# V, U and S matmuls on 16-bit operands: x, w_in, v and w_spatial as float16 hi and lo behind scales worked out on the chip

## The chip, the core and the metric

The kernel runs on one core of a Trainium2 chip. A core has a matrix engine (TensorE, in the profile PE for matmuls and PEld for weight loads), a vector engine (VectorE, DVE), a scalar engine (ScalarE, ACT), a general engine (GpSimd, POOL) and a queue engine (SyncE, SP) that issues loads and stores. Each engine works through its own instructions in order, and waits on semaphores for the others. The metric is the device time of one execution in microseconds, as the median of several.

## The reference, cut to what matters

For eight batches, eight heads, 576 positions and a head width of 64, an attention with two parts is computed, and its result goes through a gated block:

```python
q_d, k_d, v_d = means of q, k, v over groups of 4 positions      # 144 positions
out_up    = repeat(softmax(q_d k_d^T / 8) v_d, 4)                # per head
out_local = softmax(where(|i-j| < 4, q k^T / 8, -1e9)) v         # a narrow band
x = (out_up + out_local) as (576, 512) per batch

h = relu(x @ w_in)                       # w_in 512 x 1024
u, v = h[:, :512], h[:, 512:]
v_n = (v - mean(v)) / sqrt(var(v) + 1e-6)           # per position
v_s = w_spatial @ v_n + b_spatial[:, None]          # w_spatial 576 x 576
out = (u * v_s) @ w_out                             # w_out 512 x 512
```

Inputs and output are float32; w_in and w_out come as float64 and are rebuilt on the chip from their integer words.

## The kernel before

**Attention.** One unit of work is a pair of heads; each of the eight batches has four pairs (`attention(n)`, n from 0 to 31). A pair loads q and k (L515) and v in overlapping windows (L521, L523), sums q and k over four positions (sum, L531 and L534), computes banded scores (S, L563, with the mask added as a bfloat16 matmul, L556), maximum, difference, exponential (L604), sum, reciprocal and norm (L608), transposes (L616) and values (AV, L696). Beside it runs the part on means: scores (L628), exponential (L637), norm (normd, L649 on ScalarE or L651 elsewhere), transposes (L664), values (L682). The mean of v is added up by DMAs that accumulate, issued by POOL (L504). Both parts meet in xf (L706, L708), which is split into x: hi = xf rounded (xhi, L713), lo = xf - hi (xlo, L715).

**Gated block.** `gated(b)` works on the x of a batch's four pairs. All its operands are held as two float32r tiles, hi and lo, and every product is three matmuls (hi hi, hi lo, lo hi). V (L742, and L747 for the last 64 positions): 128 positions by 512 columns, 12 matmuls a piece; then relu (L759), mean and variance (L751 to L753), the reciprocal root as a power on POOL (rstd, L769), apply (L756), vhi (L773) and vlo (L775, L781). U (L796): 128 features by 256 or 320 positions, 12 matmuls, relu into u (L799). S (L814, L816, L817): w_spatial times normalised v, 14 matmuls of 256 or 320 columns with the bias in the last, then gate (L825: u times S), ghi and glo (L827, L821). O (L844, L849): the gated values times w_out, 512 columns, copied out (L854) and stored.

**Weights.** 17 pieces are loaded at the start through two staging places `stg` (L391), which are handed out in the order V half of w_in (4), U half (4), w_spatial (5 and the bias), w_out (4). A float64 piece is rebuilt in six steps on VectorE, ScalarE and, for some, POOL (L406 to L431; the last is m3); hi and lo are then made at once (L379, L382).

**Order.** `Plan.run` writes out one order for each engine ahead of time: it lists the operations with planned durations, and always takes, of those that can start soonest (within NEAR ns), the one of lowest rank. Ranks are pair numbers plus constants per kind, three each (batch 0, batch 1, later): RANK, MRANK, WRANK. ON holds, by pair or piece, which engine does a movable operation (D VectorE, P POOL, A ScalarE; beyond its end the last letter holds). Places (`places`) are buffers; an operation that needs one waits until an earlier user is done. Where the plan leaves TensorE idle in the first 110 us it puts in bfloat16 matmuls without use (warm, L882). Nothing is reordered while the kernel runs.

Of the kernel before, what the change touches and what calls it, by code (L numbers as in the profile page):

```python
# [76 lines left out]
class Plan:  # L77
# [54 lines left out]
    def run(self, near=150.0, stay=0.0, dma=(1500.0, 4.2, 500.0), emit=True):  # L132
# [16 lines left out]
        while left:  # L149
# [89 lines left out]
RANK = {"load": [-6.425, 5.791, -0.091],  # L239
        "tv": [-13.62, 1.562, -8.346],  # L240
        "sum": [7.232, 2.664, -2.313],
        "S": [-5.456, -8.108, -3.65],
        "E": [-2.935, 8.439, 4.083],
        "N": [-20.365, 3.051, 3.136],
        "T": [3.06, 5.617, -6.295],
        "Sd": [-18.648, -4.028, 1.939],
        "Nd": [-2.732, 2.402, -1.457],
        "Td": [7.722, -5.93, 1.317],
        "AVd": [-13.128, 1.0, 1.083],
        "AV": [-1.585, -10.971, -1.682],  # L250
        "X": [-1.109, -4.0, 4.59]}
# [12 lines left out]
NEAR = 120.124  # L264
STAY = 7.582
# [14 lines left out]
def tile_kernel(ctx, tc, qk, vw, v4, w_in, wT, bsp, w_out, out, emit=True):  # L280
# [51 lines left out]
    win = const.tile([P, NC, 2, 2 * FF], F32R, name="win")  # L332
    wsp = const.tile([P, NT, 2, S], F32R, name="wsp")
    wsp_hh = const.tile([P, S], F32R, name="wsp_hh")
    wsp_lb = const.tile([P, S], F32R, name="wsp_lb")
    wo = const.tile([P, NF, 2, E], F32R, name="wo")
    sel = const.tile([P, 1], F32, name="sel")
    vt2 = const.tile([P, FF], F32R, name="vt2")
# [4 lines left out]
    plan.tag("stg", [stg[:, 0], stg[:, 1]])  # L343
# [5 lines left out]
    places("v", 3, [P, NW, D], F32)  # L349
# [27 lines left out]

    def split(dst_hi, dst_lo, src, scale, toks, rank, n, key):
        plan.op("ACT", 25 + act(n), lambda: nc.scalar.activation(dst_hi, src(), AF.Copy, scale=scale),  # L379
                r=toks, w=[("whi", key)], rank=rank, name="whi")  # L380
        plan.op("DVE", dve(n),
                lambda: nc.vector.scalar_tensor_tensor(dst_lo, src(), scale, f(dst_hi), op0=ALU.mult, op1=ALU.subtract),  # L382
# [3 lines left out]
    def fetch(parts, rank, kb):  # L386
        t = plan.buf("stg")
# [7 lines left out]
    def piece64(src, dst_hi, dst_lo, rank, key):  # L395

        t = fetch([(src, 0)], rank, 512)
        eb, mb = plan.buf("row"), plan.buf("row")
# [28 lines left out]
        def m3():  # L427
            if pr.eng == "POOL":
                nc.gpsimd.tensor_tensor(mb.ap, mb.ap, eb.ap, op=ALU.mult)
            else:  # L430
                nc.vector.scalar_tensor_tensor(mb.ap, mb.ap, 2.0**-20, eb.ap, op0=ALU.mult, op1=ALU.mult)  # L431
# [15 lines left out]
    def piece_tail(rank):  # L447
# [4 lines left out]
        def go():  # L452
            nc.scalar.copy(wsp_hh, t.ap[:, :S])
# [474 lines left out]
```

## Time and profile before

| | us |
|---|---|
| median of 3 runs | 614.08 |
| lowest and highest | 610.75 and 616.07 |
| the profiled execution | 617.94 |
| its span, first to last instruction | 616.0 |

The profile is of one execution. Its page gives busy time by engine, slices over the span, the chain of work that ended last, and groups of instructions named by line, engine and tile. A line such as `282.73 2.80 PE pmc L742 x12` of the chain says: from 282.73 us on, for 2.80 us, twelve matmuls of line 742 into tile pmc. In brackets behind an instruction stands how long its engine was idle before it, and who ended the wait. The mean granted TensorE clock of the execution was 0.983 of full speed.

### The profile page before, as it was taken

What the parts mean: (1) busy time and instruction counts of PE and PEld (TensorE: products, weight loads), DVE (VectorE), ACT (ScalarE), POOL (GpSimd) and SP (SyncE); (2) the same over time, 40 slices, a digit from 0 to 9 for tenths busy, and PEclk for the clock granted to TensorE, in tenths of its full rate; (3) what the DMA queues carried; (4) which work ended last, traced back from release to release, by engine and by line L of the source; (5) the groups of instructions that cost most, each with busy time, mean ns of one, the idle gap of its engine ahead of it and who ended that gap; (6) DMA issues with size and microseconds to landing.
All of it is one profiled execution on the core that took longest, in us unless ns stands there. A gap on an engine that the chain in (4) does not pass through costs nothing.

```text
span 616.0 us, 14561 instructions
## 1 busy us (share of the span) xinstructions
PE 590.8 (96%) x5987; PEld 518.0 (84%) x5987; DVE 400.7 (65%) x915; ACT 309.5 (50%) x793; POOL 183.0 (30%) x185
## 2 busy tenths in 40 slices
PE   6688888999999999999999999999999999999997
PEld 2556777898999889898999889898899889898895
DVE  5899779894696477478547857478557857135230
ACT  2666566764564446445635646444545545324221
POOL 2552441035322243114512343113522233114100
PEclk9889979999999999999999999999999999999999
DMA  9886652253234502336022622226112300000102
GB/s 261 248 209 147 156 168 92 82 151 58 78 101 88 173 14 62 95 98 144 14 65 78 194 49 61 79 87 156 20 58 95 117 9 24 18 18 2 52 1 77
DMA packets 37382, 56.95 MB, mean 92 GB/s; under 512 B 3650, under 2 KB 24130, under 8 KB 37316
## 3 DMA queue, kind: packets, MB, share of 16 engines
q1 hardware_dynamic: 35012, 48.94, 25.3%
q0 software_dynamic: 2304, 7.08, 7.4%
q8 instruction: 47, 0.77, 0.5%
q14 instruction: 19, 0.16, 0.1%
HBM read 46.57 MB, written 9.44 MB: 91 GB/s over the span
## 4 chain that ended last, share of the span: by engine, by line
PE 85%; DVE 7%; ACT 3%; DMA 2%; issue 1%; POOL 1%; SPq 0%; ACTq 0%; POOLq 0%
PE pmc L844 6%; PE pmb L814 5%; PE pmb L796 4%; PE pmd L796 4%; PE pmd L814 4%; PE pma L814 4%; PE pma L844 4%; PE pmd L742 4%; PE pma L742 4%; PE pmc L814 3%; PE pmc L796 3%; PE pma L796 3%; PE pmb L844 3%; PE pmb L742 3%; PE pmc L742 3%; PE pmd L844 2%
## 5 line engine op out<-in xcount | busy, mean ns | idle before, releaser
L844 PE MATMUL pmc<-wo,ga 128*128 128x512 f32 x132 | 33.0, 399 | 0.0
L814 PE MATMUL pmb<-wsp,vha 128*128 128x320 f32 (+1 forms) x204 | 30.8, 299 | 0.0
L814 PE MATMUL pma<-wsp,vha 128*128 128x256 f32 (+1 forms) x204 | 30.4, 297 | 0.0
L814 PE MATMUL pmd<-wsp,vha 128*128 128x256 f32 (+1 forms) x192 | 29.4, 304 | 0.0
L844 PEld LDWEIGHTS pmc<-wo,ga 128*128 128x128 f32 x132 | 24.3, 188 | 5.9 <-issue 0.6
L814 PEld LDWEIGHTS pmb<-wsp,vha 128*128 128x128 f32 x204 | 28.5, 188 | 0.1
L814 PEld LDWEIGHTS pma<-wsp,vha 128*128 128x128 f32 x204 | 28.0, 188 | 0.2 <-issue 0.2
L814 PEld LDWEIGHTS pmd<-wsp,vha 128*128 128x128 f32 x192 | 27.4, 196 | 0.5 <-issue 0.4
L651 POOL TENSOR_TENSOR edb<-edb,smdb 96x432 f32<-96x432 f32 x13 | 16.9, 1298 | 28.7 <-DVE smdb L642 23.6
L814 PE MATMUL pmc<-wsp,vha 128*128 128x256 f32 (+1 forms) x168 | 25.2, 299 | 0.0
L651 POOL TENSOR_TENSOR eda<-eda,smda 96x432 f32<-96x432 f32 x12 | 13.9, 1158 | 31.5 <-DVE smda L642 16.7
L814 PEld LDWEIGHTS pmc<-wsp,vha 128*128 128x128 f32 x168 | 23.1, 189 | 0.1
L844 PE MATMUL pma<-wo,ga 128*128 128x512 f32 x84 | 21.1, 400 | 0.0
L504 POOL DMA_DIRECT2D tvb<-v_dram x12 | 10.8, 903 | 33.7 <-DMA tvb<-v_dram 28.7
L504 POOL DMA_DIRECT2D tva<-v_dram x12 | 10.6, 884 | 33.0 <-DMA tva<-v_dram 23.1
L715 POOL TENSOR_TENSOR xa<-xfa,xa 128x576 fp32r<-128x576 f32 x7 | 10.2, 1460 | 33.4 <-ACT xa L713 33.4
L882 PE MATMUL pma<-mask_b,mask_a 128*128 128x512 bf16 x51 | 16.5, 457 | 3.2 <-DVE mask_a L329 3.2
L844 PEld LDWEIGHTS pma<-wo,ga 128*128 128x128 f32 x84 | 15.3, 188 | 3.5 <-issue 0.4
L582 DVE TENSOR_TENSOR sa<-sa,mxa 128x640 f32<-128x640 f32 x12 | 17.4, 1452 | 0.3
L715 POOL TENSOR_TENSOR xf<-xfa,xf 128x576 fp32r<-128x576 f32 x3 | 4.3, 1427 | 43.8 <-ACT xf L713 43.8
L594 DVE TENSOR_REDUCE smb<-sb 128x10 f32<-128x640 f32 x16 | 13.0, 814 | 4.5 <-ACT sb L604 4.2
L775 POOL TENSOR_TENSOR vha<-rowd,vha 128x512 fp32r<-128x512 f32 x9 | 12.1, 1348 | 12.2 <-ACT vha L773 12.2
(561 smaller groups left out, 1803.1 us busy)
## 6 DMA issues: line engine op xcount, KB each, us to landing
qka<-qk_dram SPq DMA_DIRECT2D x16, 576.0 KB, 4.0
qkb<-qk_dram SPq DMA_DIRECT2D x16, 576.0 KB, 6.2
stg<-w_in_dram SPq DMA_DIRECT2D x8, 512.0 KB, 5.2
tva<-v_dram POOLq DMA_DIRECT2D x12, 288.0 KB, 4.9
tvb<-v_dram POOLq DMA_DIRECT2D x12, 288.0 KB, 4.7
out_dram<-rowb SPq DMA_DIRECT2D x11, 256.0 KB
va<-vw_dram SPq DMA_DIRECT2D x11, 192.0 KB, 2.7
vb<-vw_dram SPq DMA_DIRECT2D x11, 192.0 KB
```

What stands on the lines that cost most here:

```text
L504: plan.op("POOL", 850, lambda r=r: nc.gpsimd.dma_start(t.ap, v4[b, r], accum_op=ALU.add), w=[t], rank=rank + 2.0 + 0.3 * r, kb=288, name="tv")
L582: nc.vector.tensor_tensor(s.ap, s.ap, mx.ap[:, :, None].broadcast_to([P, NW, 64]), op=ALU.subtract)
L594: nc.vector.tensor_reduce(sm.ap, s.ap, axis=AX.X, op=ALU.add)
L651: side(nd).tensor_tensor(ed.ap, ed.ap, smd.ap[:96, :, None].broadcast_to([96, 3, G]), op=ALU.mult)
L715: plan.op(xl, 0, lambda: side(xl).tensor_sub(x.ap[:, 1, :], xf.ap, f(x.ap[:, 0, :])), r=[xf, x.sub(0)], w=[x.sub(1)], rank=R["X"], name="xlo")
L742: nc.tensor.matmul(ps.ap, xs[c].ap[:, i, t * P:(t + 1) * P], win[:, c, j, FF:], start=(c == 0 and (i, j) == (0, 0)), stop=(c == NC - 1 and ...
L775: plan.op(vl, 0, lambda: side(vl).tensor_sub(vh.ap[:, t, 1, :], vr.ap, f(vh.ap[:, t, 0, :])), r=[vr, vh.sub(t, 0)], w=[vh.sub(t, 1)], rank ...
L796: nc.tensor.matmul(ps.ap[:, :n], win[:, c, i, ft * P:(ft + 1) * P], xs[c].ap[:, j, HA[h]:HA[h + 1]], start=(c == 0 and (i, j) == (0, 0)), ...
L814: nc.tensor.matmul(ps.ap[:, :n], vh.ap[:, c, i, fs], wsp[:, c, j, hs], start=(c == 0 and (i, j) == (0, 0)), stop=False)
L844: nc.tensor.matmul(ps.ap, g.ap[:, c, o1:o1 + P], wo[:, c, j, :], start=(c == 0 and (i, j) == (0, 0)), stop=(c == NF - 1 and i == 1))
L882: nc.tensor.matmul(ap.rearrange("p (j k) -> p j k", k=64), mask_a, mask_b[:, None, :].broadcast_to([P, 8, 64]), start=True, stop=True)
```

## The change

- win, wsp and the tail tiles of w_spatial, the normalised v (vh, vt, vt2) and x become float16, hi and lo. w_out and the gated values stay float32r. The number and shape of the matmuls stay.
- Each of the three matrices and, per batch, x get a scale that is a power of two. For a matrix, ScalarE sums the absolute values of each row of each piece (wabs); for x it sums those of the pair's v windows (vabs). `bound` then takes the maximum over the 128 partitions with a `partition_all_reduce` on POOL, and five small VectorE operations turn its exponent into a scale and an inverse. The scale multiplies hi and lo as they are made; the inverse goes into the relu of V and U and into gate. Normalised v gets its factor 1024 through the reciprocal root (variance times 2^-20).
- Hi and lo of a matrix are made when all of its pieces are summed. Rebuilt pieces wait in places of their own (mb 6, wst 5, bias 1), and stg has four places.
- A batch's four v loads are put in at its first pair, with seven places; from batch 1 on each waits for the exp of the pair four before it. The first load of the mean of v waits for an exp of the batch before.
- xlo is on VectorE for every pair; ON has other letters for sum, m3, mask, norm, normd and vlo. All ranks, NEAR and STAY are other numbers. The planner's landing time of POOL's loads and its durations of V, U and S are changed. xf and xtail get two places, x seven, row five.

```diff
-                stop = moved + dma[2]
+                stop = t + dma[0] + 2 * o.kb * dma[1] + 2 * dma[2] if o.eng == "POOL" else moved + dma[2]
...
-WRANK = {"WV": [-8.825, 0.01],
-        "WU": [3.09, 0.206],
-        "WSP": [-1.275, 0.06],
-        "WO": [-16.539, 7.189]}
+WRANK = {"WV": [-1.602, 0.026],
+        "WU": [6.345, 0.522],
+        "WSP": [4.854, 0.053],
+        "WO": [13.75, 0.145]}
...
-ON = {"sum": "DDPPDDDPD",
-        "m3": "DDPPPPDDDDDD",
-        "mask": "TTTTTTTTD",
-        "norm": "PDDDDPDDD",
-        "xlo": "PDPDPDDPP",
-        "normd": "APAAAAADP",
-        "vlo": "PDPPPPPPPPP"}
+ON = {"sum": "DPDPPDPPD",
+        "m3": "DDDDPPDDDDDD",
+        "mask": "TTTTTTDDD",
+        "norm": "PDPDDDPPD",
+        "normd": "DDAAAPAPA",
+        "vlo": "PDDDPDPPPPD"}
...
-    win = const.tile([P, NC, 2, 2 * FF], F32R, name="win")
-    wsp = const.tile([P, NT, 2, S], F32R, name="wsp")
+    win = const.tile([P, NC, 2, 2 * FF], F16, name="win")
+    wsp = const.tile([P, NT, 2, S], F16, name="wsp")
...
-    plan.tag("stg", [stg[:, 0], stg[:, 1]])
+    more = const.tile([P, 2, 2 * FF], F32, name="more")
+    plan.tag("stg", [stg[:, 0], stg[:, 1], more[:, 0], more[:, 1]])
...
-    places("v", 3, [P, NW, D], F32)
+    places("v", 7, [P, NW, D], F32)
...
-    places("x", 6, [P, 2, S], F32R)
-    places("vh", 1, [P, NT, 2, FF], F32R)
+    places("x", 7, [P, 2, S], F16)
+    places("vh", 1, [P, NT, 2, FF], F16)
...
+    def bound(t, k, toks, tok, rank, up, fac, low):
+        def act1():
+            nc.gpsimd.partition_all_reduce(t()[:, 10:10 + k], t()[:, :k], P, bass_isa.ReduceOp.max)
+        def scales():
+            e, sc, iv = (t().bitcast(I32)[:, i:i + 1] for i in (7, 8, 9))
+            nc.vector.tensor_reduce(t()[:, 7:8], t()[:, 10:10 + k], axis=AX.X, op=ALU.max)
+            nc.vector.tensor_scalar(e, e, 0x7F800000, None, op0=ALU.bitwise_and)
+            nc.vector.tensor_scalar(e, e, -1.0, -low * 2.0**23, op0=ALU.mult, op1=ALU.min)
+            nc.vector.tensor_scalar_add(sc, e, (268.0 - up) * 2**23)
+            nc.vector.tensor_scalar(iv, e, -1.0, (up - 14.0 + fac) * 2**23, op0=ALU.mult, op1=ALU.add)
+        plan.op("POOL", 460, act1, r=toks, w=[tok], rank=rank, name="bound")
+        plan.op("DVE", 520, scales, w=[tok], rank=rank, port=True, name="scale")
...
+    for i, k in enumerate(later):
+        toks = []
+        for c, (done, t, rank, n) in enumerate(later[k]):
+            plan.op("ACT", 75 + act(n), lambda i=i, c=c, t=t, n=n: nc.scalar.activation(junk[:, :n], t.ap[:, :n], AF.Abs, accum_out=sw[:, i, c:c + 1]),
+                    r=[t], w=[("sum", k, c)], rank=rank, name="wabs")
+            toks.append(("sum", k, c))
...
+        bound(lambda i=i: sw[:, i], len(toks), toks, ("sw", i), rank, 0.0, -10.0 if k == "WSP" else -20.0, 50.0)
+        for done, t, rank, n in later[k]:
+            wtok[k] += done()
...
+        plan.op("SP", 180, go, w=[vb], after=exp_of[NP * b - NP + p:][:1] if b else (), rank=NP * b + 0.2 * p + RANK["vload"][min(b, 2)], kb=320, name="v")
+        plan.op("ACT", 640, lambda: nc.scalar.activation(junk, vb.ap.rearrange("p w d -> p (w d)"), AF.Abs, accum_out=sx.ap[:, p:p + 1]),
+                r=[vb], w=[sx.sub(p)], hold=[iv], rank=NP * b + 0.2 * p + RANK["vabs"][min(b, 2)], name="vabs")
...
+        bound(lambda: sx.ap, NP, [sx.sub(p) for p in range(NP)], sx.sub(8), rank, 1.0, 0.0, 30.0)
...
-        plan.op("ACT", 567, lambda: nc.scalar.copy(x.ap[:, 0, :], xf.ap), r=[xf], w=[x.sub(0)], rank=R["X"], name="xhi")
-        xl = Way("xlo", n, D=("DVE", 669, True), P=("POOL", 1380, True))
+        plan.op("ACT", 567, lambda: nc.scalar.activation(x.ap[:, 0, :], xf.ap, AF.Copy, scale=sx.ap[:, 8:9]), r=[xf, sx.sub(8)], w=[x.sub(0)],
+                rank=R["X"], name="xhi")
+        plan.op("DVE", 669, lambda: nc.vector.scalar_tensor_tensor(x.ap[:, 1, :], xf.ap, sx.ap[:, 8:9], x.ap[:, 0, :], op0=ALU.mult, op1=ALU.subtract),
+                r=[xf, x.sub(0), sx.sub(8)], w=[x.sub(1)], rank=R["X"], port=True, name="xlo")
...
-                plan.op("PE", 12 * 232, mm, r=xr + wtok["WV"], w=[ps], hold=[vr, vh], rank=rank, lag=PEL + 60, mode="F", name="V")
-                plan.op("ACT", 490, lambda: nc.scalar.activation(vr.ap, ps.ap, AF.Relu), r=[ps], w=[vr], rank=rank - EVICT, name="relu")
+                plan.op("PE", 12 * 216, mm, r=xr + wtok["WV"], w=[ps], hold=[vr, vh], rank=rank, lag=PEL + 60, mode="F", name="V")
+                plan.op("ACT", 490, lambda: nc.scalar.activation(vr.ap, ps.ap, AF.Relu, scale=iv.ap[:, :1]), r=[ps, iv], w=[vr], rank=rank - EVICT, name="relu")
...
-            plan.op("PE", 14 * (118 if h == 0 else 147), mm, r=vtok + wtok["WSP"], w=[ps], hold=[g, u], after=first, rank=rank, lag=PEL, mode="F", name="SP")
-            plan.op("DVE", 341 if h == 0 else 407, lambda: nc.vector.tensor_tensor(u.ap[:, :n], ps.ap[:, :n], u.ap[:, :n], op=ALU.mult),
+            plan.op("PE", 14 * (109 if h == 0 else 136), mm, r=vtok + wtok["WSP"], w=[ps], hold=[g, u], after=first, rank=rank, lag=PEL, mode="F", name="SP")
+            plan.op("DVE", 341 if h == 0 else 407, lambda: nc.vector.scalar_tensor_tensor(u.ap[:, :n], ps.ap[:, :n], sw[:, 2, 9:10], u.ap[:, :n], op0=ALU.mult, op1=ALU.mult),
```

More of the change, by code (lines that the diff above doesn't have):

```diff
@@ L233, in run @@
         return end
[L239 to L251, printed above, removed]
@@ L264 @@
-NEAR = 120.124
-STAY = 7.582
-WARM = 110000.0
-ON = {"sum": "DDPPDDDPD",
-        "m3": "DDPPPPDDDDDD",
-        "mask": "TTTTTTTTD",
-        "norm": "PDDDDPDDD",
-        "xlo": "PDPDPDDPP",
-        "normd": "APAAAAADP",
-        "vlo": "PDPPPPPPPPP"}
+RANK = {"load": [-18.015, 18.278, -10.967],
+        "vload": [14.653, 29.047, -44.789],
+        "vabs": [5.148, -21.054, 8.726],
+        "tv": [-17.596, 44.748, -14.513],
+        "sum": [-9.361, 54.365, 31.844],
+        "S": [0.467, -43.049, -2.863],
+        "E": [-4.708, -17.424, 17.239],
+        "N": [-0.954, 16.443, -17.879],
+        "T": [-2.112, -1.883, -0.175],
+        "Sd": [4.249, -16.814, -16.415],
+        "Nd": [0.272, 10.582, 13.87],
+        "Td": [2.387, -5.202, -2.239],
+        "AVd": [12.798, -6.379, 1.899],
+        "AV": [-14.369, -16.422, 0.473],
+        "X": [5.26, -13.708, 14.218]}
@@ L397, in piece64 @@
         t = fetch([(src, 0)], rank, 512)
-        eb, mb = plan.buf("row"), plan.buf("row")
+        eb, mb = plan.buf("row"), plan.buf("mb")
         def words():
@@ L454, in piece_tail, with zero, ab @@
-        plan.op("ACT", 573, go, r=[t], w=[("hh",)], rank=rank, name="hh")
-        plan.op("DVE", 668, lambda: nc.vector.tensor_sub(wsp_lb[:TAIL], t.ap[:TAIL, :S], f(wsp_hh[:TAIL])),
-                r=[t, ("hh",)], w=[("lb", 0)], rank=rank, port=True, name="lb")
+        later["WSP"].append((lambda: tail_done(t, tb, rank, rows), t, rank, S))
+        k = NT + 1
+        def zero():
+            nc.vector.memset(sw[:, 2, k:k + 1], 0.0)
+        def ab():
+            nc.scalar.activation(junk[rows, :S], tb.ap[rows, :S], AF.Abs, accum_out=sw[rows, 2, k:k + 1])
@@ new lines, in piece_tail, with tail_done @@
+        plan.op("DVE", 60, zero, w=[("zero",)], rank=rank, name="zero")
+        plan.op("ACT", 580, ab, r=[tb, ("zero",)], w=[("sum", "WSP", k)], rank=rank, name="wabs")
+    def tail_done(t, tb, rank, rows):
+        sc = sw[:, 2, 8:9]
+        tok = ("sw", 2)
+        plan.op("ACT", 573, lambda: nc.scalar.activation(wsp_hh, t.ap, AF.Copy, scale=sc), r=[t, tok], w=[("hh",)], rank=rank, name="hh")
+        plan.op("DVE", 668, lambda: nc.vector.scalar_tensor_tensor(wsp_lb[:TAIL], t.ap[:TAIL], sc[:TAIL], wsp_hh[:TAIL], op0=ALU.mult, op1=ALU.subtract),
+                r=[t, ("hh",), tok], w=[("lb", 0)], rank=rank, port=True, name="lb")
@@ L459, in b1 @@
         def b1():
-            nc.scalar.copy(t.ap.bitcast(F32R)[rows, :S], tb.ap[rows, :S])
+            nc.scalar.activation(tb.ap[rows, :S], tb.ap[rows, :S], AF.Copy, scale=sc[rows])
+            nc.scalar.copy(bh[rows], tb.ap[rows, :S])
         def b2():
@@ L603, in attention @@
                 r=[ps, mx], w=[s], rank=R["E"] - EVICT, name="sub")
-        plan.op("ACT", 643, lambda: nc.scalar.activation(s.ap, s.ap, AF.Exp, scale=1.0 / 8.0), w=[s], rank=R["E"], name="exp")
+        exp_of.append(plan.op("ACT", 643, lambda: nc.scalar.activation(s.ap, s.ap, AF.Exp, scale=1.0 / 8.0), w=[s], rank=R["E"], name="exp"))
         plan.op("DVE", 736, total, r=[s], w=[sm], rank=R["N"], name="sum")
@@ L766, in v_piece @@
                         r=[ps], w=[tmp], rank=rank - EVICT, name="vadd")
-                plan.op("ACT", 526, lambda: nc.scalar.activation(vr.ap[:r], tmp.ap[:r], AF.Relu), r=[tmp], w=[vr], rank=rank, name="relu")
+                plan.op("ACT", 526, lambda: nc.scalar.activation(vr.ap[:r], tmp.ap[:r], AF.Relu, scale=iv.ap[:r, :1]), r=[tmp, iv], w=[vr], rank=rank, name="relu")
             plan.op("DVE", 1010, stats, r=[vr], w=[st], rank=rank, name="stats")
```

137 lines of the change are left out of this document (86 added, 51 removed).

## The prediction

> **What bounds the kernel now.** I read the shares and slices on the page first.
>
> ```profile
> PE 590.8 (96%) x5987; PEld 518.0 (84%) x5987; DVE 400.7 (65%) x915; ACT 309.5 (50%) x793; POOL 183.0 (30%) x185
> PEclk9889979999999999999999999999999999999999
> ```
>
> TensorE is busy 96% of 616.0 us, at full clock after a disturbed start. Next, busy time by stage (columns: stretch, length, then PE, PEld, DVE, ACT, POOL, clock, DMA share, GB/s): two stretches of the start, then one whole batch.
>
> ```profile
> 20.00:40.00 20.00, 14.61 (x222) 9.77 (x222) 18.11 (x41) 13.11 (x40) 12.28 (x11) 0.88 0.85 224
> 40.00:60.00 20.00, 17.90 (x246) 12.21 (x244) 19.32 (x43) 14.45 (x38) 7.67 (x6) 1.00 0.62 153
> 282.73:352.68 69.95, 69.95 (x742) 62.98 (x741) 47.07 (x109) 35.91 (x94) 22.04 (x21) 1.00 0.32 88
> ```
>
> In the middle PE has no idle time in 69.95 us; in the start VectorE is the full engine (19.32 of 20). Third, the chain of waits (start us, length us, what):
>
> ```profile
> 282.73 2.80 PE pmc L742 x12
> 297.32 1.87 PE pma L747 x8
> 299.19 1.41 PE pmd L796 x12
> 302.01 1.76 PE pmb L796 x12
> 309.48 1.44 PE pmd L814 x12
> 330.16 1.77 PE pmc L814 x12
> 352.68 2.80 PE pma L742 x12
> ```
>
> The chain is PE's own order, and the V stage returns after 69.95 us. Eight such batches are 559.6 us of the 616.0; the other 56.4 are start and tail. PE's order in time shows where the first V stage begins, at 53.84, last held up by x of the fourth pair:
>
> ```profile
> 53.84 1.05 PE L742 MATMUL pmb<-win,xa 128*128 128x512 f32 x3
> 56.61 0.72 PE L742 MATMUL pmb<-win,xd 128*128 128x512 f32 x2 [0.31 <-ACT xd L713]
> ```
>
> So two prices decide: one matmul in the middle, and latency in the start.
>
> **The matmuls.** V, U and S take 16-bit operands; O (L844) and attention stay. Per piece above: 233.3 ns at 512 columns (2.80/12), 146.7 at 320 in U and 147.5 in S, 117.5 at 256 in U and 120 in S. This trace has 16-bit matmuls of its own, the mask and warm-up ones (first PE in order of time, then their durations, ns min/median/max):
>
> ```profile
> 96.42 0.43 PE L556 MATMUL paa<-mask_b,mask_a 128*128 128x320 bf16 x2
> 98.22 1.04 PE L882 MATMUL pma<-mask_b,mask_a 128*128 128x512 bf16 x4
> L882 PE MATMUL pma<-mask_b,mask_a x51: 377/381/634, 3.2 to 98.9; 128*128 128x512 bf16 x51
> L556 PE MATMUL paa<-mask_b,mask_a x12: 296/298/309, 9.1 to 96.6; 128*128 128x320 bf16 x12
> ```
>
> Four starts at 512 columns give (1040-381)/3 = 220 ns each; two at 320 give 430-298 = 132. Against 233.3 and 147 these are 0.943 and 0.90; for 256 columns, which no row has, I take the mean, 0.92, or 109. They are bf16; fp16 I price alike. Per batch V has 56 matmuls: 56 x 13.3 = 0.74 us. U and S have 48 + 56 at 320: 104 x 15 = 1.56. At 256: 48 x 8.5 + 56 x 11 = 1.02. Sum 3.33 us, times eight 26.6. Bounds: with 256 columns unimproved 18.4; with 0.90 everywhere (V 1.31, the others 1.56 and 1.24) 33. All of it counts where PE is gapless.
>
> **The other engines in the middle.** The diff puts every xlo on VectorE, from batch 2 every vlo too, and normd on ScalarE.
>
> ```profile
> L715 DVE TENSOR_TENSOR xb<-xfa,xb x1: 752/752/752, 48.0 to 48.0; 128x576 fp32r<-128x576 f32 x1
> L775 DVE TENSOR_TENSOR vha<-rowb,vha x1: 682/682/682, 69.3 to 69.3; 128x512 fp32r<-128x512 f32 x1
> 17.76 0.16 DVE L597 TENSOR_SCALAR sma<-sma 128x10 f32<-128x10 f32 x1
> L604 ACT ACTIVATE sa<-sa x16: 721/740/742, 15.6 to 491.7; 128x640 f32<-128x640 f32 x16
> L637 ACT ACTIVATION_READ_ACCUMULATOR eda<-pmc,mxda 96x1 f32 x18 | 3.5, 194 | 0.0
> L649 ACT ACTIVATE eda<-eda,smda x12: 399/402/426, 23.3 to 116.8; 96x144 f32<-96x144 f32 x12
> ```
>
> VectorE gains at most 4 x 0.75 + 4 x 0.68 + 6 small ones at 0.16 = 6.7 us a batch: 53.8 of 66.7. ScalarE gains four absolute sums at 0.74 + 0.19 and up to four normd of 3 x 0.40: 8.5, so 44.4 of 66.7. Neither becomes the bound; the cover is PE's own 66.7, and gone only if either passes it. The scale operands on relu, xhi and gate ride on instructions that exist; I price them at 0, between 0 and 0.16 each, and gaplessness hides them. The new v loads come before their use by a batch, on SP, which only issues.
>
> **The reduction on POOL.** Eleven times (three weights, eight batches) POOL reduces over the partitions. Nothing like it runs before. Below, the shortest rows at hand; as work it resembles POOL's small power operation.
>
> ```profile
> L769 POOL TENSOR_TENSOR sta<-sta,mhalf x14: 538/550/888, 63.8 to 570.1; 128x1 f32<-128x1 f32 x11, 64x1 f32<-64x1 f32 x3
> masks.py:199 POOLq MODIFY_POOL_CONFIG  x2: 8/8/8, 0.9 to 0.9; - x2
> masks.py:199 POOL TENSOR_SCALAR_AFFINE_SELECT ident<-ident x1: 292/292/292, 1.0 to 1.0; 128x128 f32<-128x128 f32 x1
> stg<-w_in_dram SPq DMA_DIRECT2D x8, 512.0 KB, 5.2
> qkb<-qk_dram SPq DMA_DIRECT2D x16, 576.0 KB, 6.2
> va<-vw_dram SPq DMA_DIRECT2D x22, 64.0 KB, 4.1
> ```
>
> The work itself I price at 0.55. But POOL configures itself (MODIFY_POOL_CONFIG) ahead of its first program, here with nothing to see: 8 ns, and the next instruction 0.1 us on. If the reduction's program and the two-input program (norm, rstd, vlo) are not held together, each reduction costs an exchange there and one back. The trace cannot show whether; one exchange lies between 0.008 and, if code is fetched like the largest loads, 6.2 us. A fetch is nearest to the weight load, so I take 5.2, or 10.4 for a pair. The Trainium skill, GPSIMD Engine Reference, section 2.1 Instruction dispatch, speaks against this change: the first call of a freshly loaded program pays some 6 us (5.95), with no instruction visible; by that figure a pair is 11.9 and the two exposed pairs below would add 3 us to the sum. The 8 ns rows neither confirm nor refute it, since there nothing may have had to be loaded.
>
> In the middle such a pair is covered. The first exchange runs while POOL awaits the sums. The second needs time between the reduction and the next rstd, the first of V (here an exp, the transposes that read it, and that rstd):
>
> ```profile
> 328.41 0.74 ACT L604 ACTIVATE sa<-sa 128x640 f32<-128x640 f32 x1 [0.38 <-DVE sa L582]
> 340.40 0.77 PE L616 MATMUL pab<-ident,sa 128*128 128x128 f32 x5
> 358.38 0.89 POOL L769 TENSOR_TENSOR stc<-stc,mhalf 128x1 f32<-128x1 f32 x1
> ```
>
> The diff releases the last v load of a batch after the fourth exp of the batch before it. Here that is the exp at 328.41, whose sa is transposed last ahead of the V stage at 352.68. It ends at 329.15; landing 4.1 (the slower of the two kinds of v transfer), absolute sum 0.93, reduction 0.55: 334.7. Until 358.4 that leaves 23.6 us for 5.2, in the order of before; the new ranks may shift it. On POOL the reduction waits for the sums, and behind it are queued the v accumulations, rstd and vlo of the tail rows; for rstd wait apply, vhi and at last S. Without the cover each batch would lose the pair, 10.4 us. I take 0.
>
> In the start there is no such room. POOL's waits there:
>
> ```profile
> 24.88 2.47 POOL L651 TENSOR_TENSOR edb<-edb,smdb 96x432 f32<-96x432 f32 x1 [3.62 <-DVE smdb L642]
> 35.67 1.78 POOL L429 TENSOR_TENSOR rowd<-rowd,rowc 128x512 f32<-128x512 f32 x1 [1.47 <-DVE rowc L416]
> 40.62 0.83 POOL L504 DMA_DIRECT2D tvb<-v_dram  x1 [3.17 <-DMA tvb<-v_dram]
> 50.28 1.27 POOL L429 TENSOR_TENSOR rowd<-rowd,rowc 128x512 f32<-128x512 f32 x1 [5.58 <-DVE rowc L416]
> ```
>
> Five reductions fall into it: three weights, batches 0 and 1. w_spatial, the V half of w_in and v of batch 0 arrive together, with four staging places and five more; I let these three share a pair, hidden by 3.62: 6.8 us exposed, since POOL's sums and norms of the first pairs queue behind it. The U half and batch 1 share a second, hidden by 5.58: 4.8. Sum 11.6.
>
> **The weights' order.** Hi and lo now wait until all of a matrix is summed.
>
> ```profile
> 38.59 0.68 DVE L382 SCALAR_TENSOR_TENSOR win<-rowd,win 128x512 fp32r<-128x512 f32 x1
> L379 ACT ACTIVATE win<-rowb x4: 623/630/635, 9.6 to 56.5; 128x512 fp32r<-128x512 f32 x4
> ```
>
> The staging places are handed out in the order V half, U half, w_spatial, w_out, so the fourth lo of the start (the row above) ends V's weights, at 39.3; the first V began at 53.84: 14.5 us lie free. The delayed chain is one absolute sum 0.82 (the hi row plus the accumulator's 0.19), reduction 0.55, five small operations 0.8, four hi at 0.63, a last lo 0.68: 5.4, against 1.3 before. Cover enough; without it 4.1. VectorE is nearly full from 20 to 60 us, and by the letters in the diff batch 0 brings it two xlo (1.5), two m3 of 512 columns (1.4 by the 0.68 row) and two normd of 432 elements (1.0, scaled from the same row) and takes off one norm (0.75 at least): +3.1. Part of it falls before 20 us or into the 2.6 us that the two stretches have free; I take 1.5, between 0 and 3.1. The remaining edits (ranks, the planner's landing time for POOL's loads, more places for x, xf, row, staging) move order alone. In the gapless middle order is worth nothing; in the start four staging places let weights land earlier, while w_out and the U half can come too late. I take 0, between -5 and +5: PE itself is idle for 5.4 and 2.1 us of those two stretches, which is what order alone could win, and I let it lose as much.
>
> **Sum.** The profiled execution took 617.9 (span 616.0 plus 1.9). 617.9 - 26.6 + 11.6 + 1.5 = 604.4. It stood 3.8 above the median of the runs, 614.1; so 601 on the median's scale, rounded up.
>
> **Rivals.** First, the exchange costs nothing: 601 - 11.6 = 589. For it the 8 ns rows; against it that they precede a program which may have been there. Second, slower: all five reductions of the start make their own pair. Place: POOL, between 18 and 70 us, with norm, sums, m3 and rstd queued behind. 5 x 10.4 = 52, less 13.8 of waits above, 38.2, instead of 11.6: 601 + 26.6 = 628. It decides from where 10 exchanges less 13.8 pass the gain of 26.6, 4 us each. For it: the kernel's planner has 460 ns for the reduction and nothing for an exchange, so nothing in its order keeps reductions together; against it, the three sets of inputs land close to one another. In the middle the same mechanism needs an exchange above 23.6 us to count. Third, the gain is given back: three pairs exposed (31.2 - 13.8 = 17.4) with 256 columns unimproved by their weight loads (18.4): 614.1 - 18.4 + 17.4 + 1.5 = 615. Against it, PEld's row for 16-bit weights, where a load of 98 ns fits into 109:
>
> ```profile
> L882 PEld LDWEIGHTS <-mask_a x51: 95/98/152, 3.2 to 98.7; 128*128 128x128 bf16 x51
> ```
>
> **Numbers.** A change of 1% (6 us) is about what a measurement of this kernel can tell from none. Forecast 0.36, first rival 0.21, slower rival 0.27, given back 0.16. Faster by over 1% (below 608) are the first two, 0.57; within 1% the gain given back, 0.16; slower 0.27. Range 584 to 633: below, the first rival less the 5 for order; above, the slower rival plus 5. The forecast's own range is 594 to 608.
>
> **What would show it.** Starts of V 66.6 us apart in the middle, L742 pieces at 2.64 us instead of 2.80, L796 at 1.58 and 1.31: the matmul term. POOL instructions before and behind the reduction several us apart with more MODIFY_POOL_CONFIG: the exchange; the first V start at 60 to 65: its exposure. PE idle between V and S would refute the cover, and an unchanged piece of 2.80 us the whole gain.

## The result and the profile after

The changed kernel takes 647.34 us (median; 646.47 to 649.81) against 615.08 before on the same chip: a ratio of 1.0541, 95% interval [1.0492, 1.059]. The forecast was 601, the range ended at 633 and the slower rival at 628.

The page of the changed kernel, shares and slices:

```profile
PE 574.3 (89%) x5991; PEld 422.4 (65%) x5991; DVE 429.4 (66%) x1033; ACT 373.4 (58%) x952; POOL 99.5 (15%) x122
...
PEclk9667879999699999899999999899989999999999
```

TensorE does less work (574.3 us, before 590.8) and stands idle for 71.8 us of its span, before 25.2. Busy time by stage (stretch, length, then PE, PEld, DVE, ACT, POOL, clock, DMA share, GB/s) for the same stretches of the start and for one batch from V to V:

```profile
20.00:40.00 20.00, 4.86 (x52) 3.50 (x52) 10.88 (x26) 10.82 (x24) 2.86 (x4) 0.54 0.95 236
40.00:60.00 20.00, 9.59 (x169) 6.44 (x165) 12.89 (x27) 13.22 (x32) 1.53 (x2) 0.84 0.42 148
319.06:388.42 69.36, 67.28 (x743) 50.55 (x742) 48.80 (x121) 43.02 (x114) 8.04 (x10) 1.00 0.31 88
```

In the start none of the compute engines is full any more, VectorE neither (10.88 of 20, before 18.11): all wait. The DMA engines are at 0.95 from 20 to 40 us, but in the first run below, without exchanges, they are at 0.99 there and the first V comes 19.4 us earlier, so they are not what holds the start up. In the middle the batch is back at 69.36 us, of which PE is busy for 67.28.

PE's order in time holds the first V stage and a stage of the middle (start, length, first operation of the line, count of pieces merged):

```profile
83.98 0.81 PE L829 MATMUL pmc<-win,xa 128*128 128x512 f16 x3
...
319.06 0.81 PE L829 MATMUL pmb<-win,xe 128*128 128x512 f16 x3
...
335.99 0.72 PE L781 MATMUL pab<-probTa,vc 64*64 64x60 f32 x33 [1.35 <-ACT probTb L703]
...
388.42 0.81 PE L829 MATMUL pmd<-win,xb 128*128 128x512 f16 x3
```

The first V starts at 83.98, 30.1 us later than before. The chain shows the cheaper matmuls, and between them engines that were not in it before:

```profile
324.22 0.17 DVE sta L841
324.39 3.21 issue
327.60 0.60 POOL sta L857
...
343.16 1.31 PE pmd L902 x12
...
349.29 1.63 PE pmd L884 x12
...
531.32 2.59 PE pmc L829 x12
```

Twelve matmuls of 256 columns take 1.31 us (109 each), of 320 columns 1.63 (136), of 512 columns 2.59 (216). And rstd on POOL is now on the path: its operand is there at 324.39, it starts at 327.60. TensorE's wait of 1.35 us at 335.99 follows between V and S, where the prediction said that idle time would refute the cover. POOL's order in time in the start shows the first two pairs of exchanges and the beginning of the third ("issue": POOL waited for nothing that the profile shows):

```profile
35.33 0.75 POOL L394 PARTITION_ALL_REDUCE sw<-sw  x2 [8.56 <-issue]
48.16 1.15 POOL L616 TENSOR_TENSOR suma<-qkb 128x576 f32<-128x576 f32 x1 [12.07 <-DVE kda L619]
55.11 0.39 POOL L394 PARTITION_ALL_REDUCE sxa<-sxa  x1 [5.80 <-DVE sma L683]
62.42 0.65 POOL L619 TENSOR_TENSOR kdb<-suma 128x288 f32<-128x288 f32 x1 [6.92 <-issue]
...
87.07 0.39 POOL L394 PARTITION_ALL_REDUCE sxb<-sxb  x1 [7.13 <-issue]
```

A reduction here is 0.39 us of work; ahead of each change of kind POOL stands idle, 6.92 to 8.56 us where nothing else is waited for. In the 12.07 row the exchange is over earlier, perhaps: kda on VectorE ended last. The same view in the middle:

```profile
280.47 0.55 POOL L394 PARTITION_ALL_REDUCE sxa<-sxa  x1 [7.75 <-ACT junk L583]
307.32 1.08 POOL L566 DMA_DIRECT2D tvb<-v_dram  x1 [26.29 <-PE pmc L932]
313.04 0.82 POOL L566 DMA_DIRECT2D tvb<-v_dram  x1 [4.64 <-DMA tvb<-v_dram]
318.44 0.83 POOL L566 DMA_DIRECT2D tvb<-v_dram  x1 [4.58 <-DMA tvb<-v_dram]
327.60 0.59 POOL L857 TENSOR_TENSOR sta<-sta,mhalf 128x1 f32<-128x1 f32 x1 [8.33 <-issue]
```

This is the reading that the prediction lacked. Between the reduction and the next rstd POOL has 26.29 us without work, and uses none of it: the exchange back to the two-input program comes after the three accumulating transfers, directly ahead of rstd, 8.33 us, and 3.2 of these delay it. When an exchange begins can be read from MODIFY_POOL_CONFIG, the instruction that stands ahead of each change of program, two at a time (those of all reductions, then those of this rstd; count, ns min/median/max, first and last start):

```profile
L394 POOLq MODIFY_POOL_CONFIG  x18: 1/4/319, 26.4 to 485.1; - x18
L857 POOLq MODIFY_POOL_CONFIG  x2: 331/331/331, 319.0 to 319.1; - x2
```

So the eleven reductions made nine changes to their program, and the change back to rstd began at 319.0, where the third transfer is issued, and not behind the reduction, which ended at 281.0. The way to the reduction was covered in the middle, as the prediction had it: its change began at 272.9, the last sum on ScalarE ended at 280.27, and the reduction started 0.2 us later.

### The profile page after: what moved, and what is told of

It is laid out like the page before. It is cut to its first block, busy times and chain, and to the rows that moved or that the text cites. A ratio compares the mean times of both kernels' runs of the same rounds, so it can differ in the third digit from the quotient of the medians.

```text
span 646.1 us, 14773 instructions
## 1 busy us (share of the span) xinstructions
PE 574.3 (89%) x5991; PEld 422.4 (65%) x5991; DVE 429.4 (66%) x1033; ACT 373.4 (58%) x952; POOL 99.5 (15%) x122
## 4 chain that ended last, share of the span: by engine, by line
PE 67%; DVE 13%; issue 8%; ACT 5%; DMA 4%; POOL 3%; SPq 0%; ACTq 0%; POOLq 0%; DVEq 0%
PE pmc L884 4%; PE pmd L902 4%; PE pmc L902 4%; PE pma L902 4%; PE pmb L932 4%; PE pmd L884 3%; PE pma L884 3%; PE pma L932 3%; PE pmb L902 3%; DMA qka<-qk_dram 3%; PE pmb L884 3%; PE pmd L932 3%; PE pmc L932 3%; PE paa L781 2%; PE paa L701 2%
## 5 line engine op out<-in xcount | busy, mean ns | idle before, releaser
L884 PEld LDWEIGHTS <-win 128*128 128x128 f16 x768 | 76.6, 101 | 25.1 <-issue 4.4
L902 PEld LDWEIGHTS <-vha 128*128 128x128 f16 x768 | 74.5, 98 | 19.9 <-issue 1.5
L902 PE MATMUL pmd<-wsp,vha 128*128 128x320 f16 (+1 forms) x204 | 27.9, 286 | 0.0
L902 PE MATMUL pmc<-wsp,vha 128*128 128x256 f16 (+1 forms) x204 | 27.6, 285 | 0.0
L902 PE MATMUL pma<-wsp,vha 128*128 128x256 f16 (+1 forms) x192 | 26.2, 286 | 0.0
L902 PE MATMUL pmb<-wsp,vha 128*128 128x256 f16 (+1 forms) x168 | 22.9, 286 | 0.0
L829 PEld LDWEIGHTS <-xa 128*128 128x128 f16 x96 | 9.5, 99 | 11.6 <-issue 0.7
L734 ACT ACTIVATE eda<-eda,smda 96x144 f32<-96x144 f32 x45 | 15.4, 407 | 1.5 <-DVE smda L727 1.4
L932 PE MATMUL pmd<-wo,gb 128*128 128x512 f32 x60 | 15.1, 401 | 0.0
L932 PE MATMUL pmb<-wo,gb 128*128 128x512 f32 x60 | 15.1, 401 | 0.0
L932 PE MATMUL pma<-wo,gb 128*128 128x512 f32 x60 | 14.9, 397 | 0.0
```

The source lines that it names most:

```text
L734: nc.scalar.activation(ed.ap[:, a, :], ed.ap[:, a, :], AF.Copy, scale=smd.ap[:96, a:a + 1])
L829: nc.tensor.matmul(ps.ap, xs[c].ap[:, i, t * P:(t + 1) * P], win[:, c, j, FF:], start=(c == 0 and (i, j) == (0, 0)), stop=(c == NC - 1 and ...
L884: nc.tensor.matmul(ps.ap[:, :n], win[:, c, i, ft * P:(ft + 1) * P], xs[c].ap[:, j, HA[h]:HA[h + 1]], start=(c == 0 and (i, j) == (0, 0)), ...
L902: nc.tensor.matmul(ps.ap[:, :n], vh.ap[:, c, i, fs], wsp[:, c, j, hs], start=(c == 0 and (i, j) == (0, 0)), stop=False)
L932: nc.tensor.matmul(ps.ap, g.ap[:, c, o1:o1 + P], wo[:, c, j, :], start=(c == 0 and (i, j) == (0, 0)), stop=(c == NF - 1 and i == 1))
```

## The experiments

**What the exchanges cost in all.** The first run keeps the order of the changed kernel and takes POOL's reduction out; the maximum over the partitions is left out with it.

```
-            nc.gpsimd.partition_all_reduce(t()[:, 10:10 + k], t()[:, :k], P, bass_isa.ReduceOp.max)
+            nc.gpsimd.tensor_tensor(t()[:, 10:10 + k], t()[:, :k], t()[:, :k], op=ALU.add)
```

> The kernel after with each reduction over the partitions replaced by an addition of the same 128x4 tile on POOL (the program that POOL's other work uses anyway). Every engine keeps its order of instructions; only MODIFY_POOL_CONFIG goes. The maximum over partitions is left out, so each partition gets a scale of its own. Theory 1 (the exchanges of POOL's program are the whole loss): 585 to 597 us, V starts 66.6 us apart in the middle, the first V start at 50 to 60 instead of 84. Theory 2 (the start is slow by itself: hi and lo wait for whole matrices, other ranks, more work on VectorE and ScalarE): 620 to 640, first V start still near 80. Theory 3 (late PE waits in the middle come from VectorE or ScalarE): gaps of 3 us before L781 once a batch stay.

Measured: 596.97 us, ratio to before 0.9678 [0.9628, 0.9728]. So eleven instructions, most of 0.4 to 0.55 us, with what surrounds them, cost 647.34 - 596.97 = 50.4 us. A batch from V to V, in the same columns as above:

```profile
343.98:410.66 66.68, 66.68 (x743) 50.42 (x741) 49.02 (x121) 43.38 (x114) 9.18 (x11) 1.00 0.35 94
```

PE is gapless again, at 66.68 us where the prediction had 66.6.

**The matmuls alone.** The kernel before with float16 operands, and none of the sums, reductions and scales.

```
-    win = const.tile([P, NC, 2, 2 * FF], F32R, name="win")
-    wsp = const.tile([P, NT, 2, S], F32R, name="wsp")
+    win = const.tile([P, NC, 2, 2 * FF], F16, name="win")
+    wsp = const.tile([P, NT, 2, S], F16, name="wsp")
...
-    places("x", 6, [P, 2, S], F32R)
+    places("x", 6, [P, 2, S], F16)
```

> The kernel before with win, wsp, vh, vt and x as float16 and nothing else: no sums, no reductions, no scales (small values of w_spatial lose places), the order of before. It measures the matmul term alone. Prediction's term: 614.1 - 26.6 = 588 us, 585 to 592, V starts 66.6 to 66.8 us apart in the middle, L742 pieces of 2.59 to 2.64 us. If VectorE, ScalarE or POOL hold PE up once it is quicker: 595 to 610 with PE gaps in the middle.

Measured: 593.28 us, 0.9648 [0.9584, 0.9711], the fastest of all. The matmul term, priced at 26.6 us, gave 21.9 by the medians and 24.8 by the spans (616.0 to 591.2).

**The reductions alone.** The kernel before, with eleven reductions whose result nobody uses.

```
+    def reduce(name, rank, r=(), after=()):
+        plan.op("POOL", 460, lambda: nc.gpsimd.partition_all_reduce(red[:, 8:12], red[:, :4], P, bass_isa.ReduceOp.max),
+                r=r, w=[("red", name)], after=after, rank=rank, name="bound")
```

> The kernel before with eleven reductions over the partitions added on POOL, of a constant tile, their result unused: three when hi and lo of a matrix are made, one per batch after the fourth exp of the batch before. Theory 1: POOL goes to and fro between two programs, 17 to 22 exchanges of 6 to 12 us, and before has more two-input work on POOL than after: 640 to 680 us, V starts 72 to 78 us apart. Theory 2: a reduction costs its 0.5 us on an engine that is 30% busy: 613 to 622.

Measured: 694.41 us, 1.1263 [1.12, 1.1326]: 79 us for eleven reductions that nobody waits for, so what waits is the two-input work behind them. Two of the start, in POOL's order, and a stretch of the same run:

```profile
43.56 0.39 POOL L495 PARTITION_ALL_REDUCE red<-red  x1 [9.75 <-issue]
50.59 0.66 POOL L547 TENSOR_TENSOR kdb<-suma 128x288 f32<-128x288 f32 x1 [6.65 <-issue]
57.07 0.39 POOL L495 PARTITION_ALL_REDUCE red<-red  x1 [5.82 <-issue]
65.05 1.25 POOL L431 TENSOR_TENSOR rowd<-rowd,rowc 128x512 f32<-128x512 f32 x1 [7.59 <-issue]
```

```profile
40.00:60.00 20.00, 5.68 (x62) 4.26 (x61) 0.00 (x0) 1.33 (x3) 1.43 (x3) 0.50 0.02 7
```

In this stretch, with three changes of program in it, VectorE does nothing for 20 us.

**Start and middle apart.** The changed kernel with the five reductions of the start replaced (the maximum left out there), the six of batches 2 to 7 kept:

```
+            if early:
+                nc.gpsimd.tensor_tensor(t()[:, 10:10 + k], t()[:, :k], t()[:, :k], op=ALU.add)
+            else:
                 nc.gpsimd.partition_all_reduce(t()[:, 10:10 + k], t()[:, :k], P, bass_isa.ReduceOp.max)
```

> The changed kernel with the five reductions of the start (three of the weights, x of batches 0 and 1) replaced by a two-input addition of the same tile, which needs no exchange; the six of the middle stay. The maximum over the partitions is left out for those five. Same order of work. If the losses of start and middle add up (50 us between the changed kernel and the one without any exchange, 19 of them before the first V): first V at about 65, distances of V in the middle as in the changed kernel (69.4-73.9), time 610 to 620. If instead the middle only suffers from what the start left behind (a queue that never catches up), the middle's distances fall to 66.7 and the time is 597-602.

Measured: 623.35 us, 1.0127 [1.0087, 1.0167], a little above the 610 to 620 expected; first V at 64.78. Against 596.97 without exchanges the six of the middle cost 26.4 us; the other 24.0 us to the changed kernel's 647.34 are put down to the five of the start, by subtraction, since no run has these alone. That the parts do not depend on each other shows in the middle: from the third V to the eighth 343.4 us pass here and 343.5 in the changed kernel.

**Is the room in the middle real?** One two-input instruction of one column directly behind each of the eleven reductions, so that the exchange back starts at once:

```
             nc.gpsimd.partition_all_reduce(t()[:, 10:10 + k], t()[:, :k], P, bass_isa.ReduceOp.max)
+            nc.gpsimd.tensor_tensor(spare, spare, mhalf, op=ALU.add)
```

> The changed kernel with one more POOL instruction directly behind each of the 11 reductions: a two-input addition of one column by 128 rows, whose result nobody reads, so that the exchange back to the two-input program begins at once and not when the next two-input instruction comes up in POOL's order. Everything else stands in the same order. Theory 1 (in the middle the exchange back is late because three accumulating transfers stand between the reduction and rstd in POOL's order, so the 23.6 us of cover are not used): the distance of V's starts in the middle falls from 69.4-73.9 to about 67-68, the idle times of TensorE of 1.4-3.7 us there go, and the time falls by 12 to 17 us from 647, to 630-635; the start (first V at 84) stays within 4 us. Rival (the middle loses to the reductions' other work, or to the lower clock by itself): 645-650, with V's distances as they were.

Measured: 648.59 us, 1.0526 [1.0496, 1.0555]. The time came out as the rival had it, but for another reason. The middle was mended as theory 1 had it: from the third V to the eighth 324.9 us pass instead of 343.5. The start lost as much again, the first V moving from 83.98 to 95.02, since reductions that had shared a pair of exchanges now had one each. So the same edit for batches 2 to 7 alone (the argument `late` is true from batch 2 on):

```
+            if late:
+                nc.gpsimd.tensor_tensor(spare, spare, mhalf, op=ALU.add)
```

> The changed kernel with the two-input addition of one column directly behind the six reductions of the middle alone (batches 2 to 7); the five of the start stay as they are. If the two effects of the run with all eleven add up (it won 18.6 us between the third and the eighth V and lost 21.2 us ahead of the third): first V at 84, distances in the middle 66.7-67.1, time 627 to 632. If the middle's gain is only lent by the later start: 640-647.

Measured: 630.96 us, 1.0234 [1.0174, 1.0293]; 16.4 us are won by adding six instructions. POOL's order in the middle:

```profile
275.03 0.55 POOL L396 PARTITION_ALL_REDUCE sxa<-sxa  x1 [7.64 <-ACT junk L587]
283.21 0.18 POOL L398 TENSOR_TENSOR spare<-spare,mhalf 128x1 f32<-128x1 f32 x1 [7.64 <-issue]
301.78 1.08 POOL L570 DMA_DIRECT2D tvb<-v_dram  x1 [18.38 <-PE pmc L936]
...
320.35 0.59 POOL L861 TENSOR_TENSOR sta<-sta,mhalf 128x1 f32<-128x1 f32 x1 [7.29 <-DVE sta L845]
```

The exchange of 7.64 us now lies in the idle time, and rstd waits for VectorE. What is left of the middle's cost is batch 2, where the next two-input instruction is not rstd but norm, and TensorE waits for it (POOL's order, then PE's):

```profile
157.27 0.39 POOL L396 PARTITION_ALL_REDUCE sxa<-sxa  x1 [6.24 <-ACT pdTa L756]
165.18 0.18 POOL L398 TENSOR_TENSOR spare<-spare,mhalf 128x1 f32<-128x1 f32 x1 [7.52 <-issue]
165.32 1.25 POOL L697 TENSOR_TENSOR sb<-sb,smb 128x640 f32<-128x640 f32 x1
```

```profile
166.63 1.33 PE L705 MATMUL paa<-ident,sb 128*128 128x128 f32 x5 [6.52 <-POOL sb L697]
```

**How much fits into the room.** A second pair behind the first, in two forms. In the first the second reduction writes x's own tile:

```
             if late:
                 nc.gpsimd.tensor_tensor(spare, spare, mhalf, op=ALU.add)
+                nc.gpsimd.partition_all_reduce(t()[:, 10:10 + k], t()[:, :k], P, bass_isa.ReduceOp.max)
+                nc.gpsimd.tensor_tensor(spare, spare, mhalf, op=ALU.add)
```

> The run before it, with a second reduction and a second one-column addition behind each of the six of the middle, so that each batch has one pair of exchanges more (some 15 us of POOL) ahead of the three accumulating transfers. If the time between the reduction and the next rstd (23.6 us in the prediction, less what the transfers need) covers it: within 2 us of the run before it. If the cover is used up by the first exchange: each of the distances in the middle grows by up to 15 us, and the time by 20 to 80 us.

Measured: 695.03 us, 1.1279 [1.1197, 1.1361]. This was not the test that was meant: the scale on VectorE now waits for the second reduction and holds VectorE's queue. Waits from 300 to 370 us (in total, times, longest):

```profile
DVE sxa L404 <- POOL sxa L399: 15.2, 1, 15.2
...
PE pmd L755 <- DVE ue L919: 5.4, 1, 5.4
```

In the second form nobody waits for it:

```
-                nc.gpsimd.partition_all_reduce(t()[:, 10:10 + k], t()[:, :k], P, bass_isa.ReduceOp.max)
+                nc.gpsimd.partition_all_reduce(spare, mhalf, P, bass_isa.ReduceOp.max)
```

> The run with the exchange directly behind the reduction from batch 2 on (630.96 us), with a second pair behind it that nobody waits for: a reduction of a constant column into the column that nobody reads, and one more addition. In the run before this one the second reduction wrote x's own tile again, so that VectorE's scale waited 15.2 us for it and held VectorE's queue; here it waits for the first reduction alone, as in the 630.96 us run. There POOL stands idle for 18.4 us between its addition and the first accumulating transfer, and a pair took 14.3 us. Theory 1 (the time between reduction and rstd hides what POOL does as long as nobody waits for it): V's distances from the third on stay at 66.7 to 67.6, and the time is 631 to 641, since batch 2's pair, which norm waits for, grows by up to 8-14 us alone or not. Rival (POOL's exchange holds up the chip by itself, by the port or the code loading): distances of 70 or more, time 650 or more.

Measured: 643.96 us, 1.0469 [1.0402, 1.0535], 13.0 more than with one pair. PE's order: two V starts of the middle, and the transpose of batch 2 that waits for norm.

```profile
180.24 1.33 PE L707 MATMUL paa<-ident,sb 128*128 128x128 f32 x5 [20.95 <-POOL sb L699]
...
326.99 0.81 PE L835 MATMUL pmb<-win,xe 128*128 128x512 f16 x3
...
393.66 0.81 PE L835 MATMUL pmd<-win,xb 128*128 128x512 f16 x3
```

From V to V it is 66.67 us, so five further pairs cost nothing where the room is. The one of batch 2, where it isn't, costs 20.95 - 6.52 = 14.4 us in full, which covers the whole difference. The rival, that an exchange holds up the chip by itself, falls.

**Other ways to the maximum.** On TensorE and VectorE in place of POOL (transpose, maximum, a matmul that spreads it), with an order of the planner's own:

```
-            nc.gpsimd.partition_all_reduce(t()[:, 10:10 + k], t()[:, :k], P, bass_isa.ReduceOp.max)
+            nc.tensor.transpose(ps[:k], t()[:, :k], ident)
...
+            nc.vector.tensor_reduce(t()[:k, 10:11], ps[:k], axis=AX.X, op=ALU.max)
...
+            nc.tensor.matmul(ps[:, :1], t()[:k, 10:11].broadcast_to([k, P]), one[:k], start=True, stop=True)
```

> The kernel after with the maximum over partitions made without POOL: PE transposes the sums, VectorE takes the maximum of each column, a matmul against a column of ones adds these up and spreads them to all partitions (a bound at most four to six times larger), VectorE goes on as before. The planner lays out its order anew. Theory 1: as the run without exchange, 585 to 600 us. Theory 2: 620 or more, first V start near 80. If the new small waits of PE on VectorE cost: 600 to 612.

Measured: 622.31 us, 1.0102 [1.0046, 1.0159]; first V at 80.48. Why it loses was not isolated: all eleven share one region of PSUM, and order and waits changed together. One cost is to be seen: the transpose stands in TensorE's own order, and in the start it held TensorE for 7.7 us until ScalarE's sum was there. On VectorE alone:

```
+            nc.vector.tensor_reduce(q, t()[:, :k], axis=AX.X, op=ALU.max)
+            nc.vector.tensor_copy(a, q.broadcast_to([P, 32]))
+            nc.vector.transpose(b, a)
+            nc.vector.tensor_reduce(m, b, axis=AX.X, op=ALU.max)
+            for i, o in ((0, 32), (32, 0), (64, 96), (96, 64)):
+                nc.vector.tensor_copy(q[o:o + 32], m[i:i + 32])
+            nc.vector.tensor_max(m, m, q)
+            for i, o in ((0, 64), (64, 0)):
+                nc.vector.tensor_copy(q[o:o + 64], m[i:i + 64])
+            nc.vector.tensor_max(t()[:, 7:8], m, q)
```

> The changed kernel with the maximum over the partitions taken on VectorE alone: a transpose of 32x32 blocks of a broadcast column, a reduction, and two rounds of copies between blocks of partitions, 10 small instructions in place of POOL's one. No exchange, no instruction of TensorE, no PSUM buffer that another step waits for; the planner lays the order out anew. Theory 1 (POOL's exchanges are the whole loss): 593-605, V's distances in the middle about 67, faster than the kernel before. Rival (the wait for a whole tile's maximum costs by itself, as the run with the maximum on TensorE, 622, suggests): 612-625.

Measured: 611.57 us, 0.9924 [0.99, 0.9947], 14.6 above the order without exchanges. The planner laid this order out anew, so the same instructions were put into the order of the changed kernel, with a one-column addition in POOL's place:

> The changed kernel in its own order, with POOL's reduction replaced by an addition of one column that nobody reads (two-input, so no exchange), and the maximum over the partitions taken by 11 more small instructions of VectorE in the step that works the scales out. Theory 1 (the order as such is good, 597 us without exchanges, and the run with the maximum on VectorE lost its 14 us by the order that the planner laid out): 597 plus 11 steps of about 1 us, of which the five of the start lie on the path: 598 to 604. Rival (the maximum on VectorE costs by itself, 14 us whatever the order): 608 to 614.

Measured: 611.06 us, 0.9914 [0.9875, 0.9953]. The rival holds: the order is not to blame, the maximum on VectorE costs 14 us in either. VectorE's order shows one (the lines of the maximum, then the next step's first):

```profile
33.82 0.15 DVE L403 TENSOR_REDUCE sw<-sw 128x1 f32<-128x6 f32 x1
...
35.98 0.16 DVE L412 TENSOR_TENSOR sw<-sw 128x1 f32<-128x1 f32 x1
36.18 0.15 DVE L413 TENSOR_SCALAR sw<-sw 128x1 int32<-128x1 int32 x1
```

It takes 2.36 us. From the third V on the distances are 66.7 to 66.8 us, as without any maximum; all of the loss lies ahead of it, where VectorE is the fullest engine (columns as above):

```profile
60.00:80.00 20.00, 15.27 (x128) 7.90 (x129) 18.50 (x51) 12.58 (x36) 5.85 (x6) 0.72 0.55 174
```

The third V comes 16.9 us later than without exchanges (227.29 against 210.37). Seven maxima stand ahead of it in VectorE's order, three weights and batches 0 to 3; at 2.36 us they make 16.5 of it. The first V comes 8.9 us later (73.45 against 64.59), with three maxima done and a fourth begun by then, 7.1 to 9.4. That what VectorE gets ahead of the third V counts in full, and behind it not at all, is read from this agreement and was not tested apart. These two are the fastest versions that keep scales and maximum: 0.8 to 0.9% below the kernel before and 36 us below the changed one. Float16 alone, without scales, is 18 us faster still.

**The scale's double wait.** Without exchanges V's first eviction waits for the scales of both halves of w_in. Two instructions instead of one (the maximum left out as in the first run):

```
-            nc.vector.tensor_scalar(iv.ap[:, :2], sw[:, :2, 9], sx.ap[:, 9:10], None, op0=ALU.mult)
+            nc.vector.tensor_scalar(iv.ap[:, h:h + 1], sw[:, h, 9:10], sx.ap[:, 9:10], None, op0=ALU.mult)
```

> The kernel of the changed order without exchanges (596.97 us, first V at 64.6), with one more edit: the inverse scale of V and that of U are worked out by two instructions, so that V's first eviction does not wait for the scale of U's half of w_in. The maximum over the partitions is left out. Theory 1 (the first V is late by the wait for the whole matrix and for both halves): first V comes 2 to 6 us earlier and the time is 591-596. Rival (what remains of the start is the work on VectorE and ScalarE itself, sums of absolute values and scales): within 1 us of 597.

Measured: 597.1 us, 0.9685 [0.9664, 0.9707], first V at 64.90: no difference. What the wait costs is not shown by this, since the eviction did not move: it starts at 73.04 us, and at 73.05 without the edit. In ScalarE's order the hi of a piece of the U half, which needs U's scale, stands ahead of it in both:

```profile
72.41 0.72 ACT L411 ACTIVATE win<-mbe,sw 128x512 f16<-128x512 f32 x1
73.04 0.67 ACT L848 ACTIVATE rowd<-pmc,sx2a 128x512 f32<-128x512 f32 x1
```

**The whole account,** read from the V starts in PE's order and the spans (us):

| kernel | first V | third V | third to eighth | span |
|---|---|---|---|---|
| before | 53.84 | 212.65 | 338.9 | 616.0 |
| float16 alone | 54.55 | 206.32 | 323.4 | 591.2 |
| changed, no exchange | 64.59 | 210.37 | 324.8 | 592.6 |
| exchange in the middle only | 64.78 | 218.81 | 343.4 | 619.7 |
| changed | 83.98 | 245.11 | 343.5 | 646.1 |
| exchange behind reduction, from batch 2 | 84.87 | 246.94 | 325.4 | 629.9 |
| exchange behind reduction, all eleven | 95.02 | 266.30 | 324.9 | 648.7 |
| second pair behind the first | 83.78 | 260.33 | 324.5 | 642.4 |
| maximum on VectorE, changed order | 73.45 | 227.29 | 324.3 | 609.1 |

In medians: 615.2 - 21.9 (matmuls) + 3.7 (sums, scales and order) + 26.4 (exchanges of batches 2 to 7) + 24.0 (exchanges of the start) = 647.4. Each term is the difference of two runs in a row, so the sum closes by itself and proves nothing; what bears it out are the distances in the table.

## Why the prediction was wrong

**The matmuls** held: 216, 136 and 109 ns against 220, 132 and 109. Five batches gained 338.9 - 323.4 = 15.5 us, 3.1 each where 3.33 stood; 21.9 to 24.8 us arrive of 26.6.

**The exchange** was seen as a mechanism, and the two programs are indeed not held together: that uncertain point of the prediction came out on its expensive side. Its size was too small: 5.2 us, where the POOL rows above that end in "issue" show 5.82 to 9.75, most of them 6.5 to 8.6. The upper bound of 6.2 did not hold it, since a large load was taken as the worst case.

**The cover in the middle** is the step that failed, and the dearest: "The second needs time between the reduction and the next rstd", 23.6 us, so 0. The first exchange of the pair was indeed covered. For the second the time was there, 26.29 us idle in the row above, and with the exchange put into it nothing is lost (324.5 to 325.4 us from the third V to the eighth). But having time is not using it. The exchange starts when the instruction that needs the other program comes up in POOL's order, and between the reduction and rstd stood the v accumulations, which the prediction had named as queued there and did not follow up. So rstd came late, 3.2 us in the chain above, and from the third V on each batch lost 3.7 us on average, 18.7 in all, which is more than the matmuls gained in the same stretch (15.5). "Above 23.6 us to count" was wrong by the same step: 8.33 us counted. For batch 2 the next two-input instruction was norm, with no room at all: with the middle's exchanges alone the first V is where it was (64.78 against 64.59), and the third 8.4 us later (218.81 against 210.37).

**The start:** two exposed pairs at 11.6 us net became 24.0. The five reductions made three pairs and not two: two weights, x of batch 0, and x of batch 1 with the third weight. The first two pairs, the four rows from 35.33 to 62.42, put the first V off by 19.4 us (83.98 against 64.59). The third starts ahead of the first V, at 80.1 us, and ends behind it; the remaining 4.6 are put down to it. The waits of 3.62 and 5.58 that were to hide part of the cost are of the kernel before. In the changed kernel two of these four turns show no wait for anything else (8.56 and 6.92, "issue"); how much the other two hid was not taken apart.

**Weights and VectorE:** 1.5 us became 3.7 (596.97 against 593.28). Without any exchange the first V is 10.0 us later than with float16 alone, of which about half is regained by the eighth. VectorE as the full engine of the start was read rightly. What makes up the 10 us was not taken apart; the run with the split scale does not settle its share either.

**The rivals:** the slower one had the right mechanism and sign and was given 0.27. It lacked the middle's 26.4 us, for the failed step above, and had five pairs in the start for 38.2 us, where three pairs cost 24.0. The two errors work against each other, so that its 628 comes within 20 us of the measured time is partly luck. The number of pairs in the start, three, was that of the rival in which the gain is given back. That the range stopped at 633 has the same cause as the failed step.

## What to carry to other kernels

Price a change of program on POOL at 6 to 10 us each way, as measured here, and look for it where the order of POOL turns from one kind of instruction to another, not at the instruction that is added. MODIFY_POOL_CONFIG shows where it starts. Room in time hides such a change only if it starts in that room: an instruction of the old kind whose result nobody reads, directly behind the new one, moves it there, and costs a pair of changes where the new ones had come in a row. And ask of each wait that you count as cover whether the work in question is next in that engine's order.

## What the runs showed of the hardware

One reduction over the partitions is mostly 0.39 to 0.55 us (one of the changed kernel took 0.84). Turning to it and back costs 5.8 to 9.8 us each way where POOL waits for nothing else. It comes at every turn: ahead of all 18 turns of the changed kernel POOL stands idle for 5.80 us or more, in the start and in the middle. The Trainium skill (GPSIMD Engine Reference, section 2.1 Instruction dispatch) has some 6 us for the first call of a freshly loaded program. The shortest row that ends in "issue", 5.82 us, agrees with that size; most are longer, and it is paid at every turn, not at the first alone.

In stretches in which the core waits TensorE's granted clock is low: 0.50 in the stretch of the reductions alone in which PE was busy 5.68 of 20 us, 0.54 in the changed kernel's 20 to 40 us. Matmuls right behind such a wait can be slower: in the changed kernel the six of L713 at 63.90 us, behind 10.85 us of waiting, took 1.73 us at a granted clock of 0.50, and six of the same shape at 50.31 us took 0.98 us at 1.00. So part of a stall can be paid again in slower matmuls; how much it is in all was not measured.
